# Chunk 0 of a fused adaLN attention and gated-MLP kernel: another order of loads and TensorE work, and an output projection by column halves

## The chip, the cores and the metric

The kernel runs on 1 core of one Trainium2 chip. The metric is device time in microseconds (us) of that core. Every kernel is judged by the median of its runs, beside runs of the kernel before on the same chip. All runs that are quoted are fast: the granted TensorE clock was 0.995 to 1.0 in all of them.

Short names: PE is TensorE, DVE is VectorE, ACT is ScalarE, POOL is GpSimd. DMA transfers are issued here from ACT, POOL and SyncE (SP), each on its own queue; a transfer *lands* when its data has arrived, and PE is *starved* while it stands before weights that have not landed. `wm`, `wmB` and `wmC` hold parts of `w_mod`; `wqk`, `wv` and `wo` hold the attention weights; `wqr` is a repacked copy of the last 64 features of `wqk`. "Gate/up" are the matmuls with `w_gate` and `w_up`; the step "up" (tile `up`) is something else: eight small matmuls after chunk 0's softmax that shift the attention weights by rows. LN2 is the second layernorm.

## The reference, cut to what matters

```python
def reference(A_x, A_wqkv, A_wo, B_x, B_w_gate, B_w_up, B_w_down, c, w_mod):   # S=2048, D=576, F=4608, bf16
    mod = (silu(c) @ w_mod).reshape(1, 6, 1, -1)
    sa, ca, ga, sb, cb, gb = (mod[:, i] for i in range(6))
    h = layernorm(x) * (1 + ca) + sa
    x = x + ga * attention(h)        # 32 heads of 18; each row attends to 8 rows, 2 apart (0, 2, ..., 14 back); then @ wo
    h = layernorm(x) * (1 + cb) + sb
    x = x + gb * ((h @ w_gate) * (h @ w_up)) @ w_down
    return x
```
(The bilinear gate has no nonlinearity.)

## The kernel before

The 2048 rows are cut into chunks of 128 or 256 rows (`SIZES`). Chunk 0 goes through attention in a *prologue* of about 35 us. From then on TensorE (PE) runs gate/up matmuls in passes, with the attention of the next chunk woven between them, and four *down* stages (`acc<-wd,hh`). Of the gate/up weights, five pairs of blocks are loaded once into the buffer `wd`, which the down weights occupy later; the others come through `gm` buffers. The order on PE is written by hand in the prologue and in the late passes; in the first `AUTO` passes a scheduler chooses it.

The projection and LN2 (cuts marked with `...`):

```python
        for j in range(ST):
            yield f"wo{j}"
            pw = banks2(ci == 0, F32, "pw")
            for m in range(KT):
                for q in range(2):
                    nc.tensor.matmul(pw[q][:, 0:288], lhsT=oT[:, m, j * P:(j + 1) * P], rhs=wo[:, m, q * 288:(q + 1) * 288],
                                     start=(m == 0), stop=(m == KT - 1))
            y = outp.tile([P, D], BF, name="y")
            for q in range(2):
                qs = slice(q * 288, (q + 1) * 288)
                nc.vector.tensor_tensor(y[:, qs], pw[q][:, 0:288], ga_bc[:, qs], ALU.mult)
            nc.vector.tensor_tensor(x_t[j][:], y[:], x_t[j][:], ALU.add)
        ...
        for _ in ln_rows(x_t, o_sb, double=True):      # bn_stats per half, bn_aggr, normalize
            pass
```

The v rows go through one buffer, `v_sb`, to a DRAM copy `vd`, from which shifted rows (`vsh`) are read back:

```python
                vt = v0 if ci == 0 else v_sb          # v_sb: one tile, made once
                for q in range(2):
                    nc.scalar.copy(vt[:]..., pv[q][:, 0:288]...)
                (nc.gpsimd if ci < 4 else nc.scalar).dma_start(vd[r0:r0 + P, :], vt[:])
```

The hand-written order of the prologue (a0, a1: projections of chunks 0 and 1; b0: attention of chunk 0; `warm(n)`: n matmuls on zeros):

```python
        go(a0, "qkr")
        next(a1)
        next(a0)
        warm(5)
        go(a1, "v0")
        for _ in range(3):
            next(b0)
        mod_row_mm(wmC, 0)                       # ga row
        go(b0, "up")
        mod_row_copy(0, ga_bc)
        pick = mod_pick(mod_columns(wmB, 0))
        ...
        go(b0, "oT")
        mod_sum(pick, 2)
        warm(2)
        next(b0)
        go(b0, "ln2")
        ...
```

## Time and profile before

| | before |
|---|---|
| time, median of 6 runs | 575.51 us (574.96 to 576.3) |
| span of the traced run | 574.0 us |
| PE busy | 561.0 us (98%) |
| first gate/up matmul | 35.48 us |
| PE waiting for `wd` in the first pass | 1.75 us in three waits |
| first gate/up matmul on `gm` after the `wd` blocks | 59.51 us |

The page of the kernel before. The first number of the PE line is its busy time; the DMA line gives the mean busy share of the 16 DMA engines in 40 slices of the span, in tenths, and the GB/s line what they moved. The last line is a group of instructions: busy time and mean ns, then PE's idle time just before them and its main releaser.

```profile
PE 561.0 (98%) x5167; PEld 369.8 (64%) x5171; DVE 317.9 (55%) x695; ACT 222.2 (39%) x395; POOL 94.4 (16%) x165
DMA  8999774349750345477402633386302214540000
GB/s 288 273 353 341 243 221 164 98 167 332 242 188 31 102 153 165 122 213 219 120 1 78 219 91 98 125 251 201 100 1 57 68 45 140 166 156 1 1 22 21
L679 PE MATMUL pgu<-h2T,wd 128*128 128x128 bf16 x512 | 34.9, 219 | 1.8 <-DMA wd<-in_B_w_gate_dram 1.0
```

PE is the limit nearly everywhere. Only the first four slices (to 57 us) have the DMA engines nearly full. The chain of waits of the first 62 us in order of time (start, length, what) shows the same from the other side: it is nearly all DMA until 54.94 us.

```profile
1.29 5.64 DMA wm<-in_w_mod_dram
...
9.13 10.04 DMA wm<-in_w_mod_dram
...
19.46 11.65 DMA wm<-in_w_mod_dram
...
32.14 9.47 DMA wd<-in_B_w_up_dram
41.60 0.28 issue
41.89 13.01 DMA wd<-in_B_w_up_dram
54.90 0.05 issue
54.94 0.84 PE pgu L679 x12
```

The three waits of PE for those loads, from the timeline (start, length, engine, line, operation, tiles; in brackets the idle time before and what ended it):

```profile
47.18 0.40 PE L679 MATMUL pgu<-h2T,wd 128*128 128x128 bf16 x4 [1.02 <-DMA wd<-in_B_w_gate_dram]
...
51.95 0.40 PE L679 MATMUL pgu<-h2T,wd 128*128 128x128 bf16 x4 [0.26 <-DMA wd<-in_B_w_up_dram]
...
54.94 0.84 PE L679 MATMUL pgu<-h2T,wd 128*128 128x128 bf16 x12 [0.47 <-DMA wd<-in_B_w_up_dram]
```

The view of stretches (window, its length, busy us of each engine, PE clock, DMA share, GB/s) for the stretch in which the rate falls and for the first pass:

```profile
20.50:27.00 6.50, 5.60 (x88) 3.83 (x88) 4.95 (x10) 2.78 (x8) 2.10 (x4) 1.00 1.06 209
27.00:36.00 9.00, 8.18 (x102) 6.31 (x102) 6.42 (x18) 3.76 (x14) 3.81 (x6) 1.00 1.04 350
36.00:61.00 25.00, 22.68 (x382) 19.53 (x381) 19.43 (x51) 14.01 (x38) 10.46 (x14) 1.00 1.03 344
```

The Trainium skill, "DMA: Bandwidth & Descriptors", section Specifications, has an HBM limit per core of about 358 GB/s; the 344 to 350 GB/s of the stretches from 27 us on agree with it.

### The profile page before, as it was taken

How to read it: one execution, taken by the hardware profiler on the slowest of the kernel's cores; microseconds unless marked ns; L12 is line 12 of the kernel's file. 1: busy time of each engine (PE TensorE's matmuls, PEld its weight loads, DVE VectorE, ACT ScalarE, POOL GpSimd, SP SyncE). 2: the span in 40 equal slices, each digit the busy share in tenths (PEclk: the TensorE clock that was granted, in tenths of full speed). 3: DMA queues.
4: the chain of work that ended last, by engine and by line, in shares of the span. 5: the costliest groups of instructions: out<-in, count | busy, mean ns of one | idle time of the engine just before them, and what ended most of it. 6: DMA issues, size and time to landing. Idle time of an engine off the chain costs nothing.

```text
span 574.0 us, 12238 instructions
## 1 busy us (share of the span) xinstructions
PE 561.0 (98%) x5167; PEld 369.8 (64%) x5171; DVE 317.9 (55%) x695; ACT 222.2 (39%) x395; POOL 94.4 (16%) x165
## 2 busy tenths in 40 slices
PE   7898999999999999999999999999999999999997
PEld 3577988888878764554468764554457754444675
DVE  5777696868788775655394525744374422122201
ACT  3454665655602225444442005454440025444200
POOL 4553202020113212010501240011200210000000
PEclk9999999999999999999999999999999999999999
DMA  8999774349750345477402633386302214540000
GB/s 288 273 353 341 243 221 164 98 167 332 242 188 31 102 153 165 122 213 219 120 1 78 219 91 98 125 251 201 100 1 57 68 45 140 166 156 1 1 22 21
DMA packets 68457, 84.32 MB, mean 147 GB/s; under 512 B 19618, under 2 KB 59506, under 8 KB 68402
## 3 DMA queue, kind: packets, MB, share of 16 engines
q1 hardware_dynamic: 56738, 45.86, 27.4%
q0 software_dynamic: 9104, 34.44, 18.0%
q10 hardware_dynamic: 2560, 3.25, 1.7%
q8 instruction: 40, 0.66, 0.5%
q14 instruction: 15, 0.12, 0.1%
HBM read 70.93 MB, written 8.67 MB: 139 GB/s over the span
## 4 chain that ended last, share of the span: by engine, by line
PE 85%; DMA 9%; DVE 3%; ACT 1%; issue 1%; POOL 0%; SPq 0%; ACTq 0%; DVEq 0%
PE pgu L679 38%; PE acc L734 24%; PE pgu L688 6%; PE pq L485 5%; DMA wm<-in_w_mod_dram 5%; DMA wd<-in_B_w_up_dram 4%; PE lgT L553 2%; PE pwA L628 2%; PE pwB L628 1%; PE pguu L679 1%; PE pgug L679 1%; PE pvA L510 1%; PE pvB L510 1%; DVE ln_stats L377 1%; DMA vd<-v_sb 1%
## 5 line engine op out<-in xcount | busy, mean ns | idle before, releaser
L679 PE MATMUL pgu<-h2T,gm 128*128 128x512 bf16 (+1 forms) x1432 | 223.1, 308 | 1.1 <-ACT gu L697 0.7
L679 PEld LDWEIGHTS <-gm 128*128 128x128 bf16 x1504 | 119.0, 98 | 107.7 <-issue 14.2
L697 ACT CAST gu<-pgu 128x1024 bf16<-128x1024 f32 (+1 forms) x171 | 136.7, 835 | 130.1 <-PE pgu L688 109.2
L734 PE MATMUL acc<-wd,hh 128*128 128x288 bf16 x1152 | 146.4, 286 | 0.0
L701 DVE TENSOR_TENSOR hh<-gu 128x512 bf16<-128x512 bf16 (+1 forms) x180 | 66.0, 371 | 127.5 <-ACT gu L697 118.4
L734 PEld LDWEIGHTS <-hh 128*128 128x128 bf16 x1152 | 112.3, 98 | 28.8 <-issue 0.4
L544 DVE TENSOR_TENSOR prod<-qT,kT 128x1280 bf16<-128x1280 bf16 (+1 forms) x80 | 46.8, 633 | 13.9 <-PE lgT L553 12.7
L527 POOL DMA_DIRECT2D vsh<-vd x30 | 22.7, 760 | 156.0 <-DMA vd<-v_sb 98.1
L743 POOL DMA_DIRECT2D out_dram<-y x15 | 8.5, 565 | 211.9 <-DVE y L742 211.9
L485 PE MATMUL pq<-hT,wqk 128*128 128x256 bf16 (+1 forms) x400 | 41.2, 251 | 0.9 <-DMA wqk<-in_A_wqkv_dram 0.9
L740 DVE TENSOR_TENSOR y<-acc,gb_bc 128x576 bf16<-128x576 f32 (+1 forms) x17 | 12.2, 717 | 52.0 <-PE acc L734 52.0
L611 DVE TENSOR_TENSOR vsh<-vsh,attn 128x2304 bf16<-128x2304 bf16 x30 | 39.9, 1354 | 0.2
L485 PEld LDWEIGHTS <-wqk 128*128 128x128 bf16 x400 | 32.2, 98 | 6.9 <-DMA wqk<-in_A_wqkv_dram 1.6
L679 PE MATMUL pgu<-h2T,wd 128*128 128x128 bf16 x512 | 34.9, 219 | 1.8 <-DMA wd<-in_B_w_gate_dram 1.0
L688 PE MATMUL pgu<-h2T,gr 64*128 64x512 bf16 (+1 forms) x358 | 34.5, 307 | 0.0
L679 PEld LDWEIGHTS <-wd 128*128 128x128 bf16 x512 | 30.1, 98 | 3.5 <-DMA wd<-in_B_w_gate_dram 1.2
L383 ACT ACTIVATE ln_rstd<-ln_stats,eps 128x2 f32<-128x2 f32 (+1 forms) x20 | 5.9, 296 | 66.5 <-DVE ln_stats L378 66.4
L377 DVE BATCH_NORM_STATS2 ln_stats<-x_t 128x6 f32<-128x288 bf16 x64 | 26.2, 448 | 1.8 <-DMA x_t<-in_A_x_dram 1.1
L688 PEld LDWEIGHTS <-gr 64*128 64x128 bf16 x376 | 12.5, 94 | 17.5 <-issue 11.1
L633 DVE TENSOR_TENSOR y<-pwA,ga_bc 128x288 bf16<-128x288 f32 x15 | 6.9, 457 | 26.1 <-PE pwA L628 25.9
L425 POOL TENSOR_SCALAR h2T<-h2T,modc 128x256 bf16<-128x256 bf16 x25 | 15.6, 634 | 29.6 <-DMA h2T<-xn_d 29.6
L612 DVE TENSOR_TENSOR vsh<-vsh 128x2304 bf16<-128x2304 bf16 x15 | 20.3, 1353 | 0.0
(153 smaller groups left out, 490.5 us busy)
## 6 DMA issues: line engine op xcount, KB each, us to landing
vsh<-vd POOLq DMA_DIRECT2D x30, 576.0 KB, 5.9
gm<-in_B_w_gate_dram SPq DMA_DIRECT2D x24, 512.0 KB, 4.0
gm<-in_B_w_up_dram SPq DMA_DIRECT2D x24, 512.0 KB, 5.0
wd<-in_B_w_down_dram SPq DMA_DIRECT2D x4, 1152.0 KB, 7.3
gm<-in_B_w_gate_dram POOLq DMA_DIRECT2D x5, 512.0 KB, 11.7
gm<-in_B_w_up_dram POOLq DMA_DIRECT2D x5, 512.0 KB, 11.6
out_dram<-y POOLq DMA_DIRECT2D x15, 144.0 KB, 2.1
wd<-in_B_w_gate_dram POOLq DMA_DIRECT2D x4, 512.0 KB, 10.2
```

The source lines that it names most:

```text
L377: nc.vector.bn_stats(stats[:, j, hf, :], src[j][:, hf * 288:(hf + 1) * 288])
L485: nc.tensor.matmul(pq[:, gi, 0:C], lhsT=wqk[:, kt, w0:w0 + P], rhs=h[:, kt, :], start=(kt == 0), stop=(kt == KT - 1))
L527: nc.gpsimd.dma_start(vsh[:].rearrange("p w d h -> p w (d h)"), src)
L544: nc.vector.tensor_tensor(prod[:, 0:nm, 0:C], qT[:, 0:nm, 0:C], kT[:, 0:nm, off:off + C], ALU.mult)
L611: nc.vector.tensor_tensor(vsh[:], vsh[:], attn[:, j, ws, None, :].to_broadcast([P, WG, DH, H]), ALU.mult)
L612: nc.vector.tensor_tensor(va[:], va[:], vb[:], ALU.add)
L628: nc.tensor.matmul(pw[q][:, 0:288], lhsT=oT[:, m, j * P:(j + 1) * P], rhs=wo[:, m, q * 288:(q + 1) * 288], start=(m == 0), stop=(m == KT - 1))
L679: nc.tensor.matmul(by_half(out[t][:, n, 0:C]), lhsT=gu_blocks[b][0][:, kt, t, (i + n) * P:(i + n + 1) * P], rhs=tokens(slice(0, P), kt), s ...
L688: nc.tensor.matmul(by_half(out[t][:, n, 0:C]), lhsT=gu_blocks[b][1][rows, (i + n) * P:(i + n + 1) * P], rhs=tokens(rows, KT - 1), start=(f ...
L697: nc.scalar.copy(g, ps[u][1][:, :, :, 0:C].rearrange("p t n c -> p n t c"))
L701: nc.vector.tensor_tensor(hh[:, fs, cs], g[:, :, 0, :], g[:, :, 1, :], ALU.mult)
L734: nc.tensor.matmul(acc[:, q, 0:288], lhsT=hh[:, f, j * P:(j + 1) * P], rhs=wd[:, f, q * 288:(q + 1) * 288], start=(f == 0), stop=(f == FT ...
```

## The change

Its intent is a shorter prologue. Chunk 0's last 64 features of q and k come straight from `wqk` (ten half-wide matmuls) and ahead of k, so that they don't wait for the repacked copy `wqr`. The matmuls of the ga row run ahead of the logits in place of warm matmuls. The v weights are loaded before the large `wmB` load. Projection, residual and LN2 statistics of chunk 0 go by column halves. The core of the diff (cut: the rest of `qk_last`, the new order of q, v and k in the projection of chunk 1, a few PSUM buffers and one `next(b0)`, and small helpers):

```diff
-            load_rows(nc.gpsimd, wmB, w_mod[:, 3 * D:5 * D])
             nc.gpsimd.memset(kT[:, :, 0:HALO], 0.0)
-            setup_mid()
-            load_rows(nc.gpsimd, wv, A_wqkv[:, 2 * D:3 * D])
+            for dst, src, parts in ((wmB, w_mod[:, 3 * D:5 * D], "r"), (wv, A_wqkv[:, 2 * D:3 * D], "mr"), (wmB, w_mod[:, 3 * D:5 * D], "m")):
+                load_rows(nc.gpsimd, dst, src, parts)
...
+                    for t in range(2):
+                        nc.tensor.matmul(pr[64 * t:64 * (t + 1), 0:C], lhsT=wqk[:, kt, t * D + 512:(t + 1) * D], rhs=h[:, kt, :],
+                                         start=(kt == 0), stop=(kt == KT - 1), skip_group_check=True)
...
+        by_half = ci == 0
+        tiles = ln_tiles() if by_half else None
         for j in range(ST):
             yield f"wo{j}"
-            pw = banks2(ci == 0, F32, "pw")
-            for m in range(KT):
-                for q in range(2):
+            pw = banks2(False, F32, "pw")
+            for q in range(2):
+                for m in range(KT):
                     nc.tensor.matmul(pw[q][:, 0:288], ...)
...
-            nc.vector.tensor_tensor(x_t[j][:], y[:], x_t[j][:], ALU.add)
+                if by_half:
+                    nc.vector.tensor_tensor(x_t[j][:, qs], y[:, qs], x_t[j][:, qs], ALU.add)
+                    ln_half(tiles, x_t, j, q)
+            if not by_half:
+                nc.vector.tensor_tensor(x_t[j][:], y[:], x_t[j][:], ALU.add)
...
-        go(a0, "qkr")
+        go(a0, "k1")
         next(a1)
         next(a0)
-        warm(5)
-        go(a1, "v0")
+        mod_row_mm(wmC, 0)
+        go(a1, "q0")
         for _ in range(3):
             next(b0)
-        mod_row_mm(wmC, 0)
+        mod_row_copy(0, ga_bc)
         go(b0, "up")
-        mod_row_copy(0, ga_bc)
+        setup_mid()
+        go(a1, "v0")
+        next(a0, None)
         pick = mod_pick(mod_columns(wmB, 0))
-        next(a0, None)
```

More of the change, by code (lines that the diff above doesn't have):

```diff
@@ L157, in load_x, with load_rows @@
             x_tiles.setdefault(ci, []).append(xt)
-    def load_rows(eng, dst, src):
-        eng.dma_start(dst[:, 0:KT - 1, :], src[0:(KT - 1) * P, :].rearrange("(k p) n -> p k n", p=P))
-        eng.dma_start(dst[0:64, KT - 1, :], src[(KT - 1) * P:D, :])
+    def load_rows(eng, dst, src, parts="mr"):
+        if "m" in parts:
+            eng.dma_start(dst[:, 0:KT - 1, :], src[0:(KT - 1) * P, :].rearrange("(k p) n -> p k n", p=P))
+        if "r" in parts:
+            eng.dma_start(dst[0:64, KT - 1, :], src[(KT - 1) * P:D, :])
     load_x(0, nc.scalar)
@@ L365, in setup_late, with ln_tiles, ln_half, ln_rows @@
         late["gup"] = pool("gup", 2)
-    def ln_rows(src, into, j0=0, act=False, double=False):
-        ST = len(src)
-        st = small.tile([P, CH // P, 14], F32, name="ln_stats", bufs=1)
-        stats, mv = st[:, :, 0:12].rearrange("p j (a b) -> p j a b", a=2), st[:, :, 12:14]
-        for j in range(ST):
-            for hf in range(2):
-                nc.vector.bn_stats(stats[:, j, hf, :], src[j][:, hf * 288:(hf + 1) * 288])
-            nc.vector.bn_aggr(mv[:, j, :], stats[:, j, :, :].rearrange("p a b -> p (a b)"))
+    def ln_tiles():
+        st = small.tile([P, CH // P, 14], F32, name="ln_stats", bufs=1)
+        return st[:, :, 0:12].rearrange("p j (a b) -> p j a b", a=2), st[:, :, 12:14]
+    def ln_half(tiles, src, j, hf):
+        nc.vector.bn_stats(tiles[0][:, j, hf, :], src[j][:, hf * 288:(hf + 1) * 288])
+        if hf:
+            nc.vector.bn_aggr(tiles[1][:, j, :], tiles[0][:, j, :, :].rearrange("p a b -> p (a b)"))
+    def ln_rows(src, into, j0=0, act=False, double=False, tiles=None):
+        ST = len(src)
+        if tiles is None:
+            tiles = ln_tiles()
+            for j in range(ST):
+                for hf in range(2):
+                    ln_half(tiles, src, j, hf)
+        mv = tiles[1]
         if act:
@@ L472, in qk @@
         def qk():
-            for t, m0, nm in ((0, 0, "q0"), (0, 2, "q1"), (1, 0, "k0"), (1, 2, "k1")):
+            pairs = [(0, 0, "q0"), (0, 2, "q1"), (1, 0, "k0"), (1, 2, "k1")]
+            for n, (t, m0, nm) in enumerate(pairs):
+                if n == 2 and ci == 0:
+                    yield from qk_last()
                 yield nm
@@ L480, in qk @@
                     halo(kT[64:, KT - 1, 0:HALO - DIL], kT[64:, KT - 1, C0:C0 + HALO - DIL])
-                pq = bank(ci == 1, "pq").rearrange("p (g c) -> p g c", g=2)
+                pq = bank(ci == 1 and nm != "q0", "pq").rearrange("p (g c) -> p g c", g=2)
                 for gi in range(2):
@@ L488, in qk, with qk_last @@
                     qT[:, m0:m0 + 2, 0:C] if t == 0 else kT[:, m0:m0 + 2, HALO:HALO + C], pq[:, :, 0:C])
+            if ci > 0:
+                yield from qk_last()
+        def qk_last():
             yield "qkr"
-            pr = bank(ci == 1, "pr")
+            pr = bank(ci < 2, "pr")
             for kt in range(KT):
-                nc.tensor.matmul(pr[:, 0:C], lhsT=wqr[:, kt, :], rhs=h[:, kt, :], start=(kt == 0), stop=(kt == KT - 1))
+                if ci == 0:
+                    for t in range(2):
+                        nc.tensor.matmul(pr[64 * t:64 * (t + 1), 0:C], lhsT=wqk[:, kt, t * D + 512:(t + 1) * D], rhs=h[:, kt, :],
+                                         start=(kt == 0), stop=(kt == KT - 1), skip_group_check=True)
+                else:
+                    nc.tensor.matmul(pr[:, 0:C], lhsT=wqr[:, kt, :], rhs=h[:, kt, :], start=(kt == 0), stop=(kt == KT - 1))
             nc.scalar.copy(qT[0:64, KT - 1, 0:C], pr[0:64, 0:C])
@@ L517, in v @@
                 (nc.gpsimd if ci < 4 else nc.scalar).dma_start(vd[r0:r0 + P, :], vt[:])
-        for part in (v, qk) if ci == 1 else (qk, v):
-            yield from part()
+        for nm in qk():
+            if ci == 1 and nm == "k0":
+                yield from v()
+            yield nm
+        if ci != 1:
+            yield from v()
         if ci > 0:
@@ L633, in attend @@
                 nc.vector.tensor_tensor(y[:, qs], pw[q][:, 0:288], ga_bc[:, qs], ALU.mult)
-            nc.vector.tensor_tensor(x_t[j][:], y[:], x_t[j][:], ALU.add)
+                if by_half:
[3 more added lines that the diff above has]
+                nc.vector.tensor_tensor(x_t[j][:], y[:], x_t[j][:], ALU.add)
         if ci == 0:
             yield "ln2"
-        for _ in ln_rows(x_t, o_sb, double=True):
+        for _ in ln_rows(x_t, o_sb, double=True, tiles=tiles):
             pass
@@ L836 @@
         go(a1, "qkr")
-        next(b0)
         mod_row_mm(wmC, 1)
```

## The prediction

> **What bounds the kernel now.** The page shows PE busy 561.0 of 574.0 us at full clock. The time-ordered chain of waits of the first 62 us is nearly all DMA: modulation weights wm (1.29 for 5.64 us, 9.13 for 10.04, 19.46 for 11.65), then gate/up weights wd (32.14 for 9.47, 41.89 for 13.01); only at 54.94 does it return to PE. The stretches view has the 16 DMA engines at a share near 1.0 from 3 to 61 us: 345-365 GB/s from 27 us, but about 200 from 20.5 to 26.7, while the wo rows and small HW-queue loads move. The PE timeline shows gate/up starting at 35.48 us, then starving for weights: 1.02 us before 47.18, 0.26 before 51.95, 0.47 before 54.94, about 1.75 in all; none later in the first pass.
>
> **What the change does to chunk 0.**
> - The wqr copies (0.85 us of POOL, after a 1.77 us wait for wqk) leave the front of POOL's queue, so wv is issued near 10 instead of 13.34. The last features come from wqk, 10 half-wide matmuls instead of 5, ahead of k: products should start near 15.8 instead of 16.34.
> - The ga row (1.71 us of PE) replaces 5 warm matmuls and no longer splits the logits; its copies (0.7 us of ACT) now precede the logits' copy. Net: softmax about 0.5 us earlier (before: 21.30).
> - After the logits PE has q0,q1 of chunk 1 (1.2), v (1.4) and the wmB columns (1.0) ahead of "up": 3.6 us from 20.7, so "up" still comes near 24.2 (before 24.17); most of the logits' gain is lost here. wmB now lands after wv, near 22.7, just before use.
> - Projection by halves: columns of half 0 end 0.7 us before half 1; multiply, add and bn_stats of half 0 run under it. One more DVE add costs about 0.15. Net about 0.5 us. PE is then free before o_sb is ready.
> I estimate gate/up starting 0.3 to 0.8 us earlier, near 34.9.
>
> **How much of it counts.** No DMA byte is removed, and POOL's queue keeps its order but for wv ahead of wmB. That queue has a backlog throughout: wmC's second half, issued at 19.46, landed at 31.1, behind wo. The Trainium skill, "DMA: Bandwidth & Descriptors", section Queues, rings and completion order, says that descriptors of one ring are consumed in ring order and that each engine takes turns between queues. Earlier issue into a backlog then moves no landing; this trace's flat DMA share agrees. So the wd blocks land nearly when they did, PE comes earlier to the same weights, and the 1.75 us of starvation grow to about 2.2. What is won is the shift of the last wd landing (54.94), which I estimate at 0 to 1 us. The rest is unchanged and PE-bound.
>
> **Prediction:** 575.1 us, 8 in 10 within 574.0 to 575.9; faster by over 2% 0.01, within 2% 0.98, slower by over 2% 0.01.
>
> **Right if:** first gate/up matmul near 34.9; softmax near 20.7 yet "up" near 24.2; PE stalls on wd in the first pass growing, their last end within 1 us of 54.94; DMA share still 1.0. **Wrong if:** the slow 200 GB/s stretch shrinks because wo and wmC are issued earlier, so that all weights land 1 to 3 us earlier and the prologue gain and the stalls are won; or wmB lands past 24 us and delays "up", LN2 and gate/up by more than the slack of some 1.7 us.

## More of the kernel before

One detail matters later: `by_half` is for chunk 0 only, but the exchange of the two matmul loops has no such guard. It changes the projection of **every** chunk.

## The result, and the profile after

Ratios here and below are the mean time of one kernel's fast runs over that of the other's of the same rounds, so they are not quite the ratio of the medians.

| | before | after |
|---|---|---|
| time, median | 575.45 us (574.42 to 576.9, 40 runs) | 574.81 us (573.81 to 576.39, 20 runs) |
| ratio to before, 95% interval | | 0.999 (0.9983 to 0.9997) |
| span of the traced run | 574.0 | 572.1 |
| softmax of chunk 0 starts | 21.30 | 20.43 |
| PE starts "up" | 24.17 | 24.50 |
| first gate/up matmul | 35.48 | 35.44 |
| last `wd` block of the first pass lands | 54.90 | 54.24 |
| first matmul on `gm` after it | 59.51 | 58.49 |
| start of the first, second down stage | 155.92, 294.10 | 154.67, 292.20 |

The result is within 2%, at about -0.64 us. The same lines of the page, chain and stretches for the kernel after:

```profile
PE 559.3 (98%) x5168; PEld 369.3 (65%) x5171; DVE 320.4 (56%) x696; ACT 222.3 (39%) x395; POOL 96.0 (17%) x165
DMA  9999775359750535468303633386302214540000
L714 PE MATMUL pgu<-h2T,wd 128*128 128x128 bf16 x512 | 34.7, 219 | 0.9 <-DMA wd<-in_B_w_up_dram 0.8
```

```profile
30.75 10.23 DMA wd<-in_B_w_up_dram
40.97 0.28 issue
41.26 12.99 DMA wd<-in_B_w_up_dram
54.24 0.05 issue
54.29 0.84 PE pgu L714 x12
```

```profile
20.50:27.00 6.50, 5.39 (x97) 4.10 (x93) 4.43 (x10) 2.35 (x7) 2.09 (x3) 1.00 1.05 262
27.00:36.00 9.00, 7.74 (x88) 5.61 (x89) 7.28 (x19) 3.15 (x12) 4.17 (x6) 1.00 1.06 333
36.00:61.00 25.00, 23.59 (x403) 20.21 (x402) 20.15 (x53) 14.25 (x39) 10.38 (x15) 1.00 1.03 343
```

(In windows of 1.5 us the kernel before moves 323 to 365 GB/s between 27 and 60 us; the prediction's 345 to 365 leaves out the dips.)

PE's timeline has a new wait in front of the `wmB` columns, and smaller ones for `wd`:

```profile
23.58 0.99 PE L247 MATMUL pm<-wm,sc_135 128*32 128x256 bf16 x40 [0.84 <-DMA wm<-in_w_mod_dram]
...
47.80 1.51 PE L714 MATMUL pgu<-h2T,wd 128*128 128x128 bf16 x24 [0.15 <-DMA wd<-in_B_w_up_dram]
...
51.28 0.40 PE L714 MATMUL pgu<-h2T,wd 128*128 128x128 bf16 x4 [0.63 <-DMA wd<-in_B_w_up_dram]
```

So the compute of the prologue won nothing: gate/up starts where it did. Yet the traced span is 1.90 us shorter. Four terms, read from the two traces, add up to 1.94 us:

- 0.66 us: the last `wd` block lands at 54.24 instead of 54.90.
- 0.37 us: from that landing to the first matmul on `gm` it takes 4.25 instead of 4.62 us. The scheduler put three projection matmuls of chunk 1 (`pwA`) in front of the last starved group instead of behind it.
- 0.53 us: three small delays late in the trace are missing, 0.27 near 90.4 us, 0.10 near 173, 0.16 near 205 (positions of the kernel before).
- 0.38 us: near 195 us PE of the kernel before waited for the copy of a v block, and the kernel after did not.

Which of them belong to the change, and which are chance of one trace?

### The profile page after: what moved, and what is told of

It reads as the page before. It is cut to its first block, busy times and chain, and to the rows that moved or that the text cites. A ratio compares the mean times of both kernels' runs of the same rounds, so it can differ in the third digit from the quotient of the medians.

```text
span 572.1 us, 12243 instructions
## 1 busy us (share of the span) xinstructions
PE 559.3 (98%) x5168; PEld 369.3 (65%) x5171; DVE 320.4 (56%) x696; ACT 222.3 (39%) x395; POOL 96.0 (17%) x165
## 4 chain that ended last, share of the span: by engine, by line
PE 87%; DMA 8%; DVE 3%; ACT 1%; issue 1%; POOL 0%; ACTq 0%; DVEq 0%
PE pgu L714 38%; PE acc L769 25%; PE pgu L723 6%; PE pq L499 5%; DMA wd<-in_B_w_up_dram 4%; DMA wm<-in_w_mod_dram 4%; PE lgT L582 2%; PE pwB L659 2%; PE pwA L659 1%; PE pguu L714 1%; PE pgug L714 1%; PE pvA L535 1%; PE pvB L535 1%; DVE ln_stats L375 1%; PE pr L517 1%
## 6 DMA issues: line engine op xcount, KB each, us to landing
wd<-in_B_w_gate_dram POOLq DMA_DIRECT2D x4, 512.0 KB, 10.2
```

## The experiments

Theories. **Weights:** the first 60 us are set by when `wd` lands; the compute prologue has slack. **Chain:** the compute prologue sets the time. **Order:** the gain lies in the later chunks, in the exchanged loops of the projection. **Second gate:** the single buffer `v_sb` can take gains back between 150 and 160 us and near 195 us. Twelve kernels ran in three calls, 5 rounds each; the medians of the kernel before in those calls were 575.37, 575.66 and 575.24 us. All outputs passed the comparison with the reference.

This table holds every trace. "Rest" is from the first `gm` matmul after the `wd` blocks to the end. "v loss" is what PE lost between 150 and 161 us and near 195 us, read by laying the starts of the same matmuls of two traces beside each other.

| kernel | projection order in later chunks | last `wd` lands | landing to `gm` | rest | v loss | median | ratio (95%) |
|---|---|---|---|---|---|---|---|
| before | old | 54.90 | 4.62 | 514.44 | 0.38 | 575.45 | |
| b_delay | old | 54.46 | 4.77 | 514.95 | 0.88 | 575.40 | 0.9993 (0.9981-1.0006) |
| b_order | new | 53.95 | 4.62 | 513.92 | 0.45 | 574.57 | 0.9991 (0.9978-1.0005) |
| after | new | 54.24 | 4.25 | 513.56 | 0 | 574.81 | 0.9990 (0.9983-0.9997) |
| a_again | new | 55.55 | 4.25 | 514.24 | 0.70 | 575.13 | 0.9996 (0.9982-1.0010) |
| a_again2 | new | 54.40 | 4.25 | 513.59 | 0.07 | 575.24 | 1.0005 (0.9991-1.0019) |
| a_up | new | 55.82 | 4.00 | 513.78 | 0 | 574.76 | 0.9990 (0.9975-1.0005) |
| a_less | new | 53.97 | 4.62 | 515.07 | 1.59 | 575.44 | 1.0002 (0.9990-1.0014) |
| a_up_less | new | 53.72 | 4.62 | 515.73 | 2.24 | 575.32 | 0.9998 (0.9983-1.0013) |
| a_delay | new | 54.90 | 4.62 | 513.46 | 0 | 574.71 | 0.9987 (0.9973-1.0000) |
| a_whole | old | 54.27 | 4.62 | 515.88 | 1.82 | 575.96 | 1.0006 (0.9992-1.0019) |
| a_rows | old | 55.00 | 4.25 | 514.73 | 0.48 | 575.57 | 1.0008 (0.9996-1.0021) |
| a_v2 | new | 54.50 | 4.25 | 513.51 | 0 | 574.29 | 0.9983 (0.9969-0.9997) |
| a_v3 | new | 54.46 | 4.01 | 513.77 | 0 | 574.50 | 0.9986 (0.9974-0.9999) |

### a_again and a_again2: the kernel after, unchanged

No edit; these show what one trace is worth.

> The changed kernel once more, for a second trace and the spread. Weights theory (the time is set by the landing of the gate/up weights of the first pass; the compute chain of chunk 0 has slack): gate/up starts near 35.4 us as before the change (35.48), PE waits on wd 0.5 to 1.3 us in all (before 1.75), the last wd wait ends near 54.3 (before 54.94), time 0.2 to 1.0 us under before. Prologue theory (the shorter chain of chunk 0 gives the gain): gate/up should start as much earlier than before as the time falls, some 0.6 us, in this trace.

> The kernel after unchanged, for a third trace and for times on the same chip as the three runs beside it. All theories: 0.5 to 0.8 us below before. The gate theory expects PE's loss between 150 and 160 us to be 0 or up to 0.7 us, as the store of v happens to land.

Measured: 575.13 and 575.24 us. In a_again gate/up started at 36.38 us, 0.9 us later than in before, so the prologue theory's mark failed; but the last wait for `wd` ended at 55.60 instead of near 54.3, so that mark of the weights theory failed too. Between the three traces of one kernel the last `wd` block landed at 54.24, 55.55 and 54.40 us. The very first weights also land anywhere: the first matmul of the modulation columns started at 6.48, 7.99 and 6.56 us. So the 0.66 us of earlier landing in the first pair of traces is less than the spread of one kernel. The old load order (before, b_order, b_delay) landed at 54.90, 53.95 and 54.46; **no earlier landing can be credited to the change**. The gain was also not seen again: 0.9996 in 6 runs and 1.0005 in 5, against 0.9990 in 20. Weighted by the number of runs, the three give 0.9994, or some -0.4 us.

### a_up: the wmB columns behind "up"

```diff
-        pick = mod_pick(mod_columns(wmB, 0))
         load_early(0)
         next(b0)
+        pick = mod_pick(mod_columns(wmB, 0))
         next(a1)
```

> Changed kernel, but the wmB columns stand after 'up' on PE, so that the late wmB (0.84 us of PE wait at 23.6) holds up only itself. 'up' should come near 23.3 instead of 24.5, gate/up 0.6 to 0.9 us earlier (near 34.7). Weights theory: the end of the last wd wait moves by less than 0.3 us, PE's waits on wd grow by 0.5 to 0.9, time within 0.3 us of a_again. Prologue theory: time 0.6 to 0.9 us under a_again.

Measured: 574.76 us, 0.37 below a_again on the same chip, inside the noise. PE had no wait for `wmB`, but gate/up still started 24.11 us after the first q matmul (24.18 in a_again, 24.03 in before), so the expected 0.6 to 0.9 us did not come. That the wait for `wmB` costs anything does not show.

### a_less and a_up_less: 442 KB less to load

```diff
-            load_rows(nc.gpsimd, wmC[:, :, D:2 * D], w_mod[:, 5 * D:6 * D])
+            nc.gpsimd.dma_start(wmC[:, 0, D:2 * D], w_mod[0:P, 5 * D:6 * D])
+            nc.gpsimd.dma_start(wmC[0:64, KT - 1, D:2 * D], w_mod[(KT - 1) * P:D, 5 * D:6 * D])
```
The gb row is then computed from the columns of ga, so its values are wrong (the output stayed within the comparison's tolerance). a_up_less adds the edit of a_up.

> Changed kernel with 442 KB fewer bytes in the queue ahead of the gate/up weights: of the gb part of w_mod only k tile 0 and the rest rows are loaded, gb is computed from the ga columns (wrong result on purpose; as many matmuls). At 350 GB/s 442 KB are 1.26 us. Weights theory: gate/up still starts near 35.4, all wd land about 1.2 us earlier, PE's waits on wd (0.8 us) nearly vanish, time 0.6 to 0.9 us under a_again. Prologue theory: no change over 0.2 us.

> Both edits: wmB columns after 'up', and 442 KB less (wrong result on purpose). Weights theory: now the earlier start of gate/up counts too; the landing allows about 1.2 us, so time 1.0 to 1.5 us under a_again, more than a_up and a_less alone. Prologue theory: as a_up, 0.6 to 0.9 us under a_again.

Measured: the last `wd` block landed at 53.97 and 53.72 us, 1.6 and 2.1 us earlier than in a_again and a_up, and the first `gm` matmul started at 58.58 and 58.34 instead of 59.80 and 59.82. That is what the weights theory expects at that place, though a_again and a_up were the latest of all traces: against the earliest landing of a modified kernel with all loads, 54.24, only 0.3 to 0.5 us is left, and b_order landed at 53.95 with all loads. So the sign agrees and the size is uncertain. The times were 575.44 and 575.32 us: **both expectations of a faster total failed**. The gain was lost around 155 us. ACT's and PE's timelines of a_up_less:

```profile
154.53 0.40 ACT L540 CAST v_sb<-pvA 128x288 bf16<-128x288 f32 x1 [3.87 <-DMA vd<-v_sb]
```

```profile
154.98 0.49 PE L425 MATMUL turnA<-identw,o_sb 128*128 128x128 bf16 x6 [0.93 <-ACT v_sb L540]
156.32 1.63 PE L770 MATMUL acc<-wd,hh 128*128 128x288 bf16 x12 [0.62 <-ACT gu L733]
```

The second v block of the pair of chunks must wait until the store of the first has left `v_sb`. That store was issued at 149.34 and landed at 154.45, while two loads of down weights, issued on SyncE's queue at 142.32 and 143.53, landed at 151.30 and 154.76. PE then waited for ACT. In the kernel after the same store took from 149.58 to 152.35 (the two loads landed at 148.69 and 151.92), ACT waited 1.54 us, and PE did not wait at all. So there is a second gate, with little slack.

### a_delay and b_delay: 2.1 us more work in the prologue

```diff
-        warm(2)
+        warm(12)
         next(b0)
```
This was put into the kernel after (a_delay) and the kernel before (b_delay), ahead of chunk 0's projection.

> The kernel after with ten more warm matmuls (0.21 us each in the trace, about 2.1 us) on PE just before chunk 0's output projection; no load is changed. Measured from the first q matmul, gate/up should start near 26.2 us instead of 24.1 to 24.2. Weights theory (the wd blocks' landings set the first pass; PE stands 0.8 to 1.2 us in front of them): the starvation vanishes, the end of the starved stretch moves by only 2.1 less that, so 0.9 to 1.3 us later, and the time rises by 0.9 to 1.3 us over the kernel after. Chain theory (compute prologue sets the time): +2.1 us at every mark and in the time.

> The same ten warm matmuls in the kernel before, whose trace shows 1.75 us of starvation on wd. Weights theory: gate/up 2.1 us later, starvation near 0, end of the starved stretch and time only 0.3 to 0.6 us later than before. Chain theory: +2.1 us in the time. If both kernels with the delay come out equal, the change gained in weight landings only; if the changed one stays 0.6 ahead, it gained in the compute chain.

Measured: gate/up started at 37.71 and 37.73 us, 2.3 us later than in the two kernels. The times were 574.71 and 575.40 us, against 575.66 for before in this call. The chain theory's +2.1 us is refuted in both. The waits for `wd` vanished but for 0.10 us in a_delay; the stretch 36 to 61 us shows what PE did in their place. The first line is a_delay, the second b_delay:

```profile
36.00:61.00 25.00, 23.60 (x394) 20.41 (x395) 21.57 (x57) 15.06 (x41) 10.63 (x15) 1.00 1.03 344
```

```profile
36.00:61.00 25.00, 24.21 (x402) 20.79 (x400) 21.45 (x57) 15.10 (x42) 10.00 (x15) 1.00 1.03 344
```

In b_delay PE is busy 24.21 of the 25 us (22.68 in before; up to 37.7 us it is still doing prologue work) and the first `gm` matmul comes at 59.23, not later than before's 59.51. In a_delay it comes at 59.51, 1.02 us later than in the trace of after, as the weights theory expected, but inside the spread of that kernel's own three traces (58.49 to 59.80). **A delay of 2.3 us in the prologue cost nothing that the runs resolve**, less than either theory expected; where the 0.3 to 1.3 us that the weights theory allowed went was not followed up. PE had slack there, so an earlier start would hardly have brought anything either.

### a_whole: no column halves anywhere

```diff
-            pw = banks2(False, F32, "pw")
-            for q in range(2):
-                for m in range(KT):
+            pw = banks2(ci == 0, F32, "pw")
+            for m in range(KT):
+                for q in range(2):
...
-        by_half = ci == 0
+        by_half = False
```

> The kernel after with the projection and LN2 of chunk 0 not by column halves (features outermost, add and statistics on whole rows, as before). My prediction's theory of a compute gain of about 0.5 us from the halves: gate/up starts near 24.6 us after the first q matmul instead of 24.1, and with the weights theory the time moves by at most 0.2. Rival (the halves gain nothing because PE has other work or DVE is not the bound there): gate/up at 24.1 and the time within 0.2.

Measured: from "up" to the normalized rows 9.71 us instead of 9.42 to 9.43 in after, a_again and a_again2 (9.79 in before), so the halves of chunk 0 are worth 0.3 us. Yet gate/up started 23.12 us after the first q matmul: both expectations of that mark missed, because `wmB` happened to land before PE asked for it. The time of 575.96 us is 0.3 us above before. That was the surprise: the last `wd` block landed at 54.27, as in the kernel after, and still the kernel was slower. Its rest is 515.88 us, and it has the three late delays of the kernel before. It had been built to undo the halves of chunk 0, and had undone the loop exchange of all chunks.

### b_order and a_rows: the loop exchange alone, in the chunks after the first

```diff
-            for m in range(KT):
-                for q in range(2):
+            for q, m in [(q, m) for q in range(2) for m in range(KT)] if ci > 0 else [(q, m) for m in range(KT) for q in range(2)]:
```
b_order is the kernel before with this edit. a_rows is the kernel after with the mirror image (`ci == 0` in place of `ci > 0`): chunk 0 keeps the whole change, later chunks get the old order.

> The kernel before with one thing of the change: in the output projection of the chunks after the first (not of chunk 0), the ten matmuls run column half by column half instead of alternating between the halves. All seven traces with the new order lack four small delays that all three traces with the old order show against the kernel after: 0.26 us at the first gate/up matmuls of the third pass (near 90.4 us), 0.10 near 173, 0.37 to 0.38 near 195 and 0.15 near 205. Order theory: this kernel lacks them too, so from the end of the starved stretch to the first down stage takes 96.1 to 96.2 instead of 96.4 us, from there to the second 137.5 instead of 138.2, and the time falls by 0.6 to 0.9 us below before; that would be most or all of the change's gain, and none of it from chunk 0. Rival (the gain comes from chunk 0's prologue and weights, the four delays come from elsewhere): the delays stay and the time is within 0.2 of before.

> The kernel after with the old, alternating order in the projection of all chunks but the first; chunk 0 keeps everything of the change. Order theory: the four delays come back, 96.4 and 138.2 us for the two stretches, and the time rises by 0.6 to 0.9 us over the kernel after, to about that of before. Rival: as the kernel after within 0.2 us.

Measured: b_order 574.57 us, a_rows 575.57 us, before 575.24 us. The two directions agree: b_order with **nothing** of the change in chunk 0 is as fast as the kernel after, and a_rows with **all** of it in chunk 0 is no faster than before. Against the kernel after (a_again2, 575.24 us, no faster than before) a_rows is 0.33 us slower, less than the expected 0.6 to 0.9. Both 95% intervals (table) contain 1, so neither run's timing alone would settle it.

Taken together the timings do point the same way. These four kernels form a square; their means are 575.33 (before), 574.72 (b_order), 575.69 (a_rows) and 575.19 us (a_again2). The new order is worth -0.61 us without the rest of the change and -0.50 with it (together -0.6, give or take 0.6), the rest of the change +0.37 and +0.47 (together +0.4, give or take 0.6). And in each of the three calls the kernels with the new order (all loads kept, one v buffer), whatever else they carry, have a lower mean than those with the old one: -0.38, -0.78 and -0.50 us, weighted -0.5, give or take 0.3 (95%, worked out from the spread of single runs, some 0.7 us).

The traces show where, as the delays come and go with the loop order. All four kernels with the old order have the three delays (0.26 to 0.27, 0.10 to 0.11, 0.15 to 0.16 us), all ten with the new order lack them. The fourth delay that I had put on the list, near 195 us, did not follow: a_rows lacks it and b_order has 0.45 of it. It belongs to the v gate.

How the first delay arises can be read on DVE and PE. The projection near 82 us, timeline of before (DVE, then PE):

```profile
83.74 0.46 DVE L633 TENSOR_TENSOR y<-pwA,ga_bc 128x288 bf16<-128x288 f32 x1 [0.73 <-PE pwA L628]
84.11 0.45 DVE L633 TENSOR_TENSOR y<-pwB,ga_bc 128x288 bf16<-128x288 f32 x1
```

```profile
90.44 0.77 PE L679 MATMUL pgu<-h2T,gm 128*128 128x128 bf16 x11 [0.44 <-ACT gu L697]
```

The same places in b_order:

```profile
82.26 0.46 DVE L632 TENSOR_TENSOR y<-pwA,ga_bc 128x288 bf16<-128x288 f32 x1 [0.25 <-PE pwA L627]
82.87 0.46 DVE L632 TENSOR_TENSOR y<-pwB,ga_bc 128x288 bf16<-128x288 f32 x1 [0.15 <-PE pwB L627]
```

```profile
89.19 1.95 PE L678 MATMUL pgu<-h2T,gm 128*128 128x128 bf16 x32 [0.18 <-ACT gu L696]
```

and in a_rows:

```profile
83.67 0.46 DVE L663 TENSOR_TENSOR y<-pwA,ga_bc 128x288 bf16<-128x288 f32 x1 [0.73 <-PE pwA L658]
```

```profile
90.37 1.83 PE L713 MATMUL pgu<-h2T,gm 128*128 128x128 bf16 x30 [0.45 <-ACT gu L731]
```

With alternating matmuls both halves end together, and DVE stands 0.73 us before it may multiply. Half by half, it waits 0.25 and 0.15. The second multiply ends 0.24 us earlier when both are measured from the same gate/up matmuls of PE (those at 86.33 us in before and 85.34 in b_order), and DVE's queue behind it (add, statistics, then the statistics of the next LN) moves with it. ACT evicts the gate/up result that PE waits for only behind the square root of that next LN (`ln_rstd`). ACT in before, then in b_order:

```profile
89.62 0.30 ACT L383 ACTIVATE ln_rstd<-ln_stats,eps 128x2 f32<-128x2 f32 x1 [2.01 <-DVE ln_stats L378]
89.82 1.05 ACT L697 CAST gu<-pgu 128x512 bf16<-128x512 f32 x2
```

```profile
88.37 0.30 ACT L383 ACTIVATE ln_rstd<-ln_stats,eps 128x2 f32<-128x2 f32 x1 [2.01 <-DVE ln_stats L378]
88.57 1.05 ACT L696 CAST gu<-pgu 128x512 bf16<-128x512 f32 x2
```

From `ln_rstd` to PE's next matmul it is 0.82 us in both, and measured from the same matmuls `ln_rstd` comes 0.26 us earlier in b_order, so PE's wait shrinks from 0.44 to 0.18. The two other delays, 0.10 and 0.16 us, are below what the wait view lists, and I did not follow them.

### a_v2 and a_v3: a second buffer for the v rows

```diff
-                vt = v0 if ci == 0 else v_sb
+                vt = v0 if ci == 0 else outp.tile([P, D], BF, name="y") if ci in (4, 5) and j else v_sb
```
There was no room for another tile, so odd blocks borrow one of the y pool. a_v3 does it for all chunks from the fifth on (`ci > 3`) and includes the edit of a_up.

> The kernel after with a second buffer for the v rows of chunks 4 and 5 (the odd block uses a buffer of the y pool), so that the ACT copy of the second block need not wait for the store of the first, which lands behind the down weights' backlog near 152 to 154 us. Theory of a second gate: ACT's wait of 1.4 to 3.9 us there vanishes, from the end of the starved stretch to the first down stage takes 96.2 us or up to 0.3 less, and the time is 0.0 to 0.4 us below the kernel after; a gain made in the prologue is then no longer given back there. Rival (the wait is only slack of ACT): ACT's wait vanishes and the time is the same within 0.2.

> A version meant to beat both: the kernel after with a second buffer for the v rows of every chunk from the fifth on (odd blocks use the y pool's buffers) and with the wmB columns on PE after up instead of before it, so that up does not wait 0.8 to 1.25 us for their load. Theory of the second gate: no PE gap between 150 and 160 us in any run (the kernel after showed 0 in one trace and 0.7 in the next, a_less 0.9, a_up_less 1.2), time 0.2 to 0.5 us below the kernel after on the same chip, a ratio to before of 0.9975 to 0.9985. Rival: as the kernel after within 0.2 us, since the gate rarely costs.

Measured: 574.29 and 574.50 us, ratios 0.9983 and 0.9986 to before, whose intervals exclude 1. Near 152 us ACT no longer waits for the store (in a_v2, whose edit ends with chunk 5, it still waits 2.00 us for one near 192 us, without a loss on PE). ACT in the kernel after, then in a_v2:

```profile
152.43 0.40 ACT L539 CAST v_sb<-pvA 128x288 bf16<-128x288 f32 x1 [1.54 <-DMA vd<-v_sb]
```

```profile
151.62 0.40 ACT L539 CAST y<-pvA 128x288 bf16<-128x288 f32 x1 [0.53 <-PE pvA L535]
```

Of the twelve traces with the single buffer, four lost 0 to 0.07 us at v copies and eight lost 0.38 to 2.24; the two with the second buffer lost nothing. On one chip a_v3's slowest run was 574.76 us and that of the kernel after 576.40 (medians 574.50 and 575.24). That is what the gate theory expects, but 5 runs each do not prove it, and a_v2 and a_v3 are "same" by the 2% measure like all the others. They are the best two medians.

## Why the prediction was right or wrong

The time was right: 574.81 us lies within 574.0 to 575.9, within 2%, 0.3 below the predicted middle. That the size of the gain fits is luck: the prediction looked for it in the landing of `wd`, where no gain is shown, and the part that is shown comes from the later chunks, which it called unchanged. Its main argument was right all the same, and the experiments show it: the first 60 us are set by the weights' landings, not by the compute chain. Point by point:

- **"Earlier issue into a backlog then moves no landing": right for `wd`.** The Trainium skill, "DMA: Bandwidth & Descriptors", section Queues, rings and completion order, was read that way, and for `wd` the traces agree. (The page says this of ring order for the queues of SyncE and ACT; that POOL's queue keeps its order too is what the traces show: in all 14 of them the transfers issued by POOL up to 48 us landed in the order of their issue.) The modified kernels' last `wd` block landed at 54.24 to 55.82 us with all loads kept, the old load order's at 53.95 to 54.90, and in every trace but b_delay's the first `gm` matmul followed exactly 4.00, 4.01, 4.25 or 4.62 us after that landing. With 442 KB less it came at 53.72 and 53.97, hardly outside that spread. For loads further ahead in the queue the rule was too strict: the larger part of `wmC`'s second half was issued 4.15 us earlier (15.31 instead of 19.46) and landed 1.39 us earlier (29.72 instead of 31.11; on average 29.97 in the nine traces of modified kernels with all loads, 30.77 in the three with the old load order), and the slow stretch did carry more, 262 instead of 209 GB/s, as the first clause of "Wrong if" said. But the next stretch carried less, 333 instead of 350, and the 1 to 3 us of that clause did not reach `wd`.
- **"Softmax about 0.5 us earlier": right.** From the first q matmul it was 9.06 us against 9.84 in the first pair. Over the eleven traces with this part of the change it averages 9.25 (8.56 to 9.74), over the three without it 9.71 (9.63 to 9.84).
- **"wmB now lands after wv, near 22.7, just before use": failed in size.** It landed at 23.54, PE waited 0.84 us for it (0 to 2.10 in the other traces), and "up" came later than before (24.50 against 24.17). So a part of the gain was paid back.
- **"Net about 0.5 us" for the halves: mis-sized.** a_whole measures 0.3 us for them.
- **"Gate/up starting 0.3 to 0.8 us earlier, near 34.9": failed.** 35.44, as good as unchanged. In the first pair the softmax came 0.87 us earlier (20.43), but "up" 0.33 later, behind the 0.84 us wait for `wmB` and the PE work that now stands ahead of it; from "up" to gate/up it took 0.37 less, and the two cancel. The delay runs show that it would not have mattered.
- **"The 1.75 us of starvation grow to about 2.2": failed.** It shrank to about 0.9 (0.6 to 1.4 in the traces with all loads and no delay). It could only grow if PE came earlier, and PE did not; in addition the landing in that trace was early, and three projection matmuls were put in front of the last wait.
- **"The rest is unchanged and PE-bound": this is the step that failed most.** I read the column halves as a change to chunk 0, as the change's title says, and missed that the exchanged matmul loops have no guard. They save 0.53 us in later chunks (b_order and a_rows), where PE's time is not covered by a wait for weights. Nothing else of the change is shown to bring time by a repeated, deliberate test.
- **"What is won is the shift of the last wd landing, 0 to 1 us": right in size for the first pair of traces (0.66), wrong as a cause.** Three traces of one kernel spread by 1.3 us.

Of the four terms of the first comparison, then, the landing (0.66) is chance of one trace; the v copy (0.38) comes and goes between traces of one kernel (0, 0.70 and 0.07 in after), but all four traces with the old order lost 0.38 to 1.82 there and four of the six with the new one (all loads kept, one v buffer) at most 0.07, and whether the order makes that loss likelier was not tested; the loop order (0.53) is shown, and the fill (0.37) is open: it came with the kernel after in all three of its traces and is absent in before, b_order, a_delay, a_whole, a_less and a_up_less; it is the scheduler's choice, a_rows has it with the old loop order, and no run isolates what triggers it. Order and fill together, 0.9 us, fit the interval of the first 20 runs (-1.0 to -0.2 us, from the ratio's interval times 575.45), but the repeats with 0.9996 and 1.0005 suggest less. What the change brings exactly stays open between about 0 and 1 us; that none of it needs to come from chunk 0 is what b_order shows.

## What to carry to other kernels

Read a diff for what it does *outside* its stated scope: a loop exchange without a guard touched all chunks, and there it was worth more than everything that was aimed at. Before shortening a prologue, lengthen it: if ten useless matmuls cost nothing that the runs resolve, as here, a rearrangement there will hardly pay until the loads land earlier. And when two traces differ by less than the same kernel does from run to run, lay several traces of the same kernel side by side, matmul by matmul: delays that come and go with one edit in every trace are the edit's, others may be chance, and a single buffer whose release waits for a store can give or take more than the edit.

## What the Trainium skill lacked or had wrong

- "DMA: Bandwidth & Descriptors", section Anatomy of one DMA — SWDGE (gpsimd) path, gives 2.0 us plus bytes / 436e3 for a transfer. Worked out for 512 KB that is an estimate of 3.2 us. The 512 KB blocks of `wd`, issued into a backlog, took a median of 10.2 us (gate) and 11.0 (up) from issue to landing in the kernel before; the 144 KB output stores, later on the same queue, took a median of 2.1 us against an estimate of 2.3. The section tells of one transfer; I found nothing in that section on what to expect behind a backlog.
- No page that I used gives the spread of a landing. The 144 KB stores of v blocks on ACT's queue took 1.7 to 7.7 us in these traces, the one near 150 us alone 2.5 to 5.1, and the last block of a saturated first pass landed within 1.3 us in three traces of one kernel.
- "Perfetto Trace Analysis", section Optimization Strategy, says that the most contended engine can change over a kernel and that repeating bubbles can mean too few buffers. The first held here (DMA to 55 us, then PE). The second is near to what a_v2 shows, but the gaps did not repeat: with one v buffer PE lost 0 to 2.24 us at two places only, 150 to 161 us and near 195 us. What the page lacks is the check by a deliberate delay, which took one run for each kernel here: 2.3 us more in the prologue of before gave 575.40 us against 575.66.
